# ConvNeXt-V2 block: recomputing three of four row groups in the second stage instead of one of two, with a fixed TensorE order

## The chip, the cores and the metric

The kernel runs on one core of one Trainium2 chip. The metric is the device time of one execution in microseconds (us), as the median of several runs; the profile is one more execution, and its span is a little shorter than the device time. The clock of TensorE is given as the share of its full clock that the profile shows as granted.

## The reference

```python
# x: [1, 512, 512, 96] bf16; dw: [3, 3, 96]; w1: [96, 384]; w2: [384, 96]; all bf16
def reference(x, dw, w1, w2, grn_gamma, grn_beta):
    # 3x3 depthwise convolution over the padded image
    for i in range(K):
        for j in range(K):
            out = out + xp[:, i:i+H, j:j+W, :] * dw[i, j][None, None, None, :]
    h = _layernorm(out, axis=-1)
    h = jnp.einsum('bhwc,ce->bhwe', h, w1)
    h = _gelu(h)
    gx = jnp.sqrt((h * h).sum(axis=(1, 2), keepdims=True) + 1e-6)   # over the whole image
    nx = gx / (gx.mean(axis=-1, keepdims=True) + 1e-6)
    h = grn_gamma * (h * nx) + grn_beta + h
    h = jnp.einsum('bhwe,ec->bhwc', h, w2)
    return x + h
```

The sum over the whole image in `gx` splits the work in two stages. The second matmul needs `gx`, so the hidden tensor (512 x 512 x 384 in bf16, about 201 MB) has to be stored in DRAM and loaded again, or computed twice.

## The kernel before

Stage one goes through the image by rows: convolution on TensorE, layer norm, first matmul, GELU, and the sum of squares on VectorE. Of each block of eight rows it stores the GELU result `g` of the first four to DRAM, and of the other four the smaller normalised input `yn`. Stage two loads `g` for the first four rows, and recomputes matmul and GELU from `yn` for the other four. Then it applies the second matmul with scaled weights `W2s` and adds x. (PE below is TensorE, PEld its weight loads, DVE VectorE, ACT ScalarE and POOL GpSimd. SP only issues DMAs; ACT and POOL issue some beside their own work. `W2s` is w2 scaled by the result of the GRN step, the global response normalisation that needs `gx`.)

```python
GB = 8; GR = 4                       # rows of a block, rows of a group
RECOMP = [(4, 4)]                    # rows 4..7 of each block are recomputed
g_dram  = dram.tile([H // GB, NCH, 128, GB, W], bf16, name="g_dram")    # NCH = 3
yn_dram = dram.tile([H, C, W], bf16, name="yn_dram")
# ... stage one (cut): convolution, layer norm, U = w1.T @ yn, gt = gelu(U), sums of gt*gt ...
            if (r % GB) in recomp_rows:
                nc.sync.dma_start(out=yn_dram[r], in_=yn[:])
# ... in stage_mlp, for each group of four rows and each j of three chunks ...
                    if (rq0 % GB) not in recomp_rows:
                        nc.sync.dma_start(out=g_dram[...], in_=gt[:])       # index cut
# ... GRN step (cut): acc -> ssq -> gx -> tot_ps -> ... -> W2s ...
        gld    = tile_pool(name="gld", bufs=4 * NCH)      # tiles of 8 KB a partition: 96 KB
        ynld   = tile_pool(name="ynld", bufs=3)
        xrpool = tile_pool(name="xr", bufs=6)
        opool  = tile_pool(name="o", bufs=6)
        psO    = tile_pool(name="psO", bufs=4, space=PSUM)
        psU2   = tile_pool(name="psU2", bufs=2, space=PSUM)
        for blk in range(H // GB):
            # load g for rows 0..3 (SP and POOL queues), yn for rows 4..7 (ACT queue)
            for i0 in range(0, n_, 2):               # recompute: 6 times two matmuls, one GELU
                for j in range(NCH):
                    U = psU2.tile([128, ni, W], f32, name="U2")
                    for i in range(ni):
                        nc.tensor.matmul(U[:, i, :], lhsT=w1_sb[...], rhs=ynt[:, i0 + i, :], ...)
                    nc.scalar.activation(out=..., in_=perm_src(U[:]), func=Gelu_apprx_tanh)
            for q in range(GB // GR):
                # xr <- x (POOL queue); xb = xr + bias on VectorE
                for sub in range(NSUB):              # 4 times: 12 matmuls, one VectorE add
                    O = psO.tile([128, GPS, C], f32, name="O")
                    # 4 x 3 matmuls O[:, gl_, :] += g_chunk.T @ W2s[:, j, :]
                    nc.vector.tensor_tensor(out=o_sb[...], in0=O[:], in1=xb[...], op=ALU.add)
                # out <- o_sb (SP and POOL queues by turns)
```

The order of the instructions on each engine is made by a scheduler from this program.

## Time and profile before

| | before |
|---|---|
| device time, median of 4 runs | 2073.48 us |
| span of the profile, mean granted clock of TensorE | 2071.3 us, 0.975 |
| end of the last sum of squares (stage one) | 1467.6 us |
| moved in 1500-2000 us | 392 GB/s |
| ACT busy in 1500-2000 us | 316 of 500 us |

The span in 40 slices (part 2 of the page; busy tenths of ACT and of the DMA engines, and the rate):

```profile
ACT  3788888888888888888888888887476666566565
...
DMA  4644546545446445455445465422799999999996
GB/s 99 161 128 125 153 134 167 150 130 137 141 142 171 139 126 152 127 151 171 129 127 153 128 158 165 126 83 109 245 399 398 395 391 397 389 387 386 386 389 266
```

The last twelve slices are stage two: the rate jumps to some 390 GB/s and stays there, while ACT has a third of its time free. The windows view gives one line for each stretch: its ends, its length, then busy time and count by engine, the granted clock, the DMA share and GB/s.

```profile
core 0: us, PE busy (x) PEld busy (x) DVE busy (x) ACT busy (x) POOL busy (x), PEclk, DMA share, GB/s
600.00:1200.00 600.00, 600.00 (x3699) 338.61 (x3697) 555.36 (x932) 525.00 (x763) 106.76 (x224) 1.00 0.52 144
1500.00:2000.00 500.00, 422.88 (x5979) 314.53 (x5976) 401.73 (x552) 315.83 (x335) 119.00 (x222) 0.97 1.03 392
```

In stage one TensorE has no idle time at clock 1.00. In stage two no compute engine is full. The chain of work that ended last (start us, length us, what) shows what stage two waits for:

```profile
1465.27 2.31 DVE junk L313 x2
...
1842.11 17.89 DMA out_dram<-o_sb
1860.06 19.10 DMA out_dram<-o_sb
1879.25 19.35 DMA out_dram<-o_sb
```

It is the sum of squares on VectorE (junk) to the end of stage one, then one output write of 18-19 us after the other. Longest waits of stage two, 1500-2000 us (in all us, times, longest us):

```profile
...
ACT gl L418 <- PE U L414: 166.3, 73, 6.1
...
DVE o_sb L438 <- DMA out_dram<-o_sb: 58.3, 31, 3.1
...
```

ACT waits for TensorE, and VectorE waits for output writes that free its tiles. The DMA issues (part 6 of the page: count, KB each, median us from issue to landing) show such transfers under load:

```profile
gl<-g_dram SPq DMA_DIRECT2D x128, 512.0 KB, 18.3
...
ynl<-yn_dram ACTq DMA_DIRECT2D x64, 384.0 KB, 14.7
out_dram<-o_sb SPq DMA_DIRECT2D x64, 384.0 KB, 18.4
```

The groups of instructions that cost most in stage two (part 5 of the page: count, busy us and mean ns of one, idle us before them):

```profile
L418 ACT ACTIVATE gl<-U 128x1024 bf16<-128x1024 f32 x384 | 363.9, 1032 | 215.6 <-PE U L414 193.4
...
L438 DVE TENSOR_TENSOR o_sb<-O,xb 128x384 bf16<-128x384 f32 x512 | 257.6, 550 | 119.6 <-DMA out_dram<-o_sb 65.3
...
L414 PE MATMUL U<-ynl,w_sb 96*128 96x512 bf16 x768 | 228.3, 386 | 34.8 <-DMA ynl<-yn_dram 22.0
```

### The profile page before, as it was taken

The numbers are of one execution on the slowest core, as the hardware profiler recorded it, in microseconds if no ns is written. First come the engines' busy times: TensorE is split into PE (matmuls) and PEld (weight loads), VectorE is DVE, ScalarE is ACT, GpSimd is POOL, SyncE is SP. The second block draws the span as 40 slices with busy tenths as digits, with TensorE's granted clock in tenths as the row PEclk, the third lists the DMA queues.
The fourth block names the chain that finished last, engine by engine and source line by source line (L and its number), as shares of the span: only waits on it lengthen the run. The fifth ranks groups of instructions, "written<-read, shape, count | busy, mean of one in ns | idle before, by whom it ended". The sixth has DMA issues, their size and how long they took to land.

```text
span 2071.3 us, 40470 instructions
## 1 busy us (share of the span) xinstructions
PE 1920.5 (93%) x15615; PEld 1162.5 (56%) x15615; DVE 1779.4 (86%) x2849; ACT 1607.4 (78%) x2181; POOL 403.8 (19%) x775
## 2 busy tenths in 40 slices
PE   7999999999999999999999999997498888788887
PEld 4555555555555555555555555552266666566665
DVE  1799999999999999999999999999697878787777
ACT  3788888888888888888888888887476666566565
POOL 0212112112112112111111121124222222222221
PEclk9999999999999999999999999997599999999999
DMA  4644546545446445455445465422799999999996
GB/s 99 161 128 125 153 134 167 150 130 137 141 142 171 139 126 152 127 151 171 129 127 153 128 158 165 126 83 109 245 399 398 395 391 397 389 387 386 386 389 266
DMA packets 432977, 430.35 MB, mean 208 GB/s; under 512 B 313904, under 2 KB 363152, under 8 KB 432784
## 3 DMA queue, kind: packets, MB, share of 16 engines
q1 hardware_dynamic: 382608, 293.53, 46.3%
q0 software_dynamic: 24576, 109.07, 13.5%
q10 hardware_dynamic: 25600, 25.17, 3.7%
q8 instruction: 122, 2.00, 0.4%
q14 instruction: 71, 0.58, 0.1%
HBM read 176.31 MB, written 176.16 MB: 170 GB/s over the span
## 4 chain that ended last, share of the span: by engine, by line
PE 68%; DMA 24%; DVE 3%; issue 3%; ACT 1%; POOL 0%; SPq 0%; POOLq 0%; ACTq 0%; DVEq 0%
PE Y L211 48%; DMA out_dram<-o_sb 21%; PE U L305 15%; PE S L232 2%; DVE junk L313 2%; DMA ynl<-yn_dram 2%; PE T L274 2%; PE O L436 1%; DMA xr<-in_x_dram 1%; DMA xT<-in_x_dram 1%; ACT gl L418 0%; PE U L414 0%; DVE xb L426 0%; DMA gl<-g_dram 0%; DVE o_sb L438 0%
## 5 line engine op out<-in xcount | busy, mean ns | idle before, releaser
L211 PE MATMUL Y<-xT,Dc 96*96 96x511 bf16 (+1 forms) x4602 | 1088.1, 380 | 14.3 <-DMA xT<-in_x_dram 14.3
L313 DVE SCALAR_TENSOR_TENSOR junk<-gt 128x2048 bf16<-128x2048 bf16 x384 | 876.4, 2282 | 78.2 <-ACT gt L310 77.5
L211 PEld LDWEIGHTS <-Dc 96*96 96x96 bf16 x4602 | 563.8, 123 | 443.7 <-DVE Dc L112 10.1
L310 ACT ACTIVATE gt<-U 128x1024 bf16<-128x1024 f32 x768 | 755.2, 1023 | 36.8 <-PE U L305 36.8
L418 ACT ACTIVATE gl<-U 128x1024 bf16<-128x1024 f32 x384 | 363.9, 1032 | 215.6 <-PE U L414 193.4
L281 POOL PARTITION_BROADCAST rbc<-RT x512 | 263.3, 619 | 1173.0 <-DVE ri L246 1060.3
L219 ACT ACTIVATE y_bf<-Y 96x512 bf16<-96x512 f32 x512 | 303.7, 593 | 181.3 <-PE Y L211 181.3
L305 PE MATMUL U<-yn,w_sb 96*128 96x512 bf16 x1536 | 428.0, 387 | 15.1 <-DVE yn L286 8.8
L436 PE MATMUL O<-W2s,gl 128*128 128x96 bf16 x6144 | 348.0, 210 | 76.0 <-DVE o_sb L438 66.1
L436 PEld LDWEIGHTS <-gl 128*128 128x128 bf16 x6144 | 315.5, 100 | 181.1 <-issue 80.7
L438 DVE TENSOR_TENSOR o_sb<-O,xb 128x384 bf16<-128x384 f32 x512 | 257.6, 550 | 119.6 <-DMA out_dram<-o_sb 65.3
L221 ACT ACTIVATE ysq<-Y 96x512 bf16<-96x512 f32 x512 | 298.7, 583 | 0.0
L414 PE MATMUL U<-ynl,w_sb 96*128 96x512 bf16 x768 | 228.3, 386 | 34.8 <-DMA ynl<-yn_dram 22.0
L305 PEld LDWEIGHTS <-w_sb 96*128 96x128 bf16 x1536 | 148.9, 99 | 183.8 <-issue 27.9
L426 DVE TENSOR_TENSOR xb<-xr,B2bc_f 128x1536 f32<-128x1536 bf16 x128 | 224.3, 1753 | 9.7 <-DMA ynl<-yn_dram 7.6
L286 DVE TENSOR_TENSOR yn<-y_bf,rbc 96x512 bf16<-96x512 bf16 x512 | 214.3, 429 | 8.2 <-POOL rbc L281 0.5
L423 POOL DMA_DIRECT2D xr<-in_x_dram x128 | 69.0, 539 | 380.6 <-DVE xb L426 269.5
L414 PEld LDWEIGHTS <-w_sb 96*128 96x128 bf16 x768 | 68.2, 99 | 57.0 <-issue 37.8
L277 DVE CAST RT<-T 128x512 bf16<-128x512 f32 x128 | 86.5, 676 | 0.3 <-PE T L274 0.3
L232 PEld LDWEIGHTS <-ysq 96*128 96x128 bf16 x2048 | 60.7, 96 | 13.5
L232 PE MATMUL S<-ones_c,ysq 96*128 96x1 bf16 x2048 | 60.3, 163 | 0.0
L243 DVE TENSOR_SCALAR var<-S 128x32 f32<-128x32 f32 x64 | 11.6, 181 | 48.8 <-PE S L232 48.8
(51 smaller groups left out, 408.9 us busy)
## 6 DMA issues: line engine op xcount, KB each, us to landing
g_dram<-gt SPq DMA_DIRECT2D x192, 512.0 KB, 3.0
gl<-g_dram SPq DMA_DIRECT2D x128, 512.0 KB, 18.3
xr<-in_x_dram POOLq DMA_DIRECT2D x128, 384.0 KB, 8.3
gl<-g_dram POOLq DMA_DIRECT2D x64, 512.0 KB, 10.1
yn_dram<-yn SPq DMA_DIRECT2D x256, 96.0 KB, 1.7
ynl<-yn_dram ACTq DMA_DIRECT2D x64, 384.0 KB, 14.7
out_dram<-o_sb SPq DMA_DIRECT2D x64, 384.0 KB, 18.4
out_dram<-o_sb POOLq DMA_DIRECT2D x64, 384.0 KB, 10.6
```

The lines of the kernel that those rows point to most:

```text
L211: nc.tensor.matmul(Y[:, oc0:oc1], lhsT=Dc[:, t, :], rhs=xT[0:C, rr + dy, oc0 + dx:oc1 + dx], start=(i == 0), stop=(i == len(taps) - 1),)
L219: nc.scalar.activation(out=y_bf[:], in_=Y[:], func=ACTF.Identity)
L221: nc.scalar.activation(out=ysq[:], in_=Y[:], func=ACTF.Square)
L281: nc.gpsimd.partition_broadcast(rbc[:], RT[32 * i:32 * i + 1, :], channels=128)
L305: nc.tensor.matmul(U[:, kk, :], lhsT=w1_sb[:, j * 128:(j + 1) * 128], rhs=yy[:], start=True, stop=True)
L310: nc.scalar.activation(out=perm_view(gt[:, :], rr0, 2), in_=perm_src(U[:]), func=ACTF.Gelu_apprx_tanh)
L313: nc.vector.scalar_tensor_tensor(out=junk[:], in0=gt[:], scalar=1.0, in1=gt[:], op0=ALU.mult, op1=ALU.mult, accum_out=acc[:, j, quad:quad ...
L414: nc.tensor.matmul(U[:, i, :], lhsT=w1_sb[:, j * 128:(j + 1) * 128], rhs=ynt[:, i0 + i, :], start=True, stop=True)
L418: nc.scalar.activation(out=perm_view(gq, (a_ + i0) % GR, ni), in_=perm_src(U[:]), func=ACTF.Gelu_apprx_tanh)
L426: nc.vector.tensor_tensor(out=xb[:], in0=xr[:], in1=B2bc_f[:, None, :].to_broadcast([128, PXP, C]), op=ALU.add)
L436: nc.tensor.matmul(O[:, gl_, :], lhsT=lhsT, rhs=W2s[:, j, :], start=(j == 0), stop=(j == NCH - 1))
L438: nc.vector.tensor_tensor(out=o_sb[:, sub * GPS:(sub + 1) * GPS, :], in0=O[:], in1=xb[:, sub * GPS:(sub + 1) * GPS, :], op=ALU.add)
```

## The change

The intent is to take bytes off the DMA engines and to give the freed time to TensorE and ACT in a fixed order. Three of four groups are recomputed instead of one of two. TensorE's order in stage two is set by hand: recompute slots (`u_slot`, two matmuls and one GELU) are spread evenly between the `O` matmuls and run 12 slots ahead. The g tiles become smaller: five groups of 3 tiles of 4 KB a partition, 60 KB instead of 96 KB.

```diff
-    RECOMP = [(4, 4)]                                  # cut: block and row bookkeeping
+    RECOMP_PATTERN = [False, True, True, True] if GR == 4 else [False]
-        gld = p2.enter_context(tc.tile_pool(name="gld", bufs=4 * NCH))
-        ynld = p2.enter_context(tc.tile_pool(name="ynld", bufs=3 * max(1, len(RECOMP))))
+        gld = p2.enter_context(tc.tile_pool(name="gld", bufs=5 * NCH))
+        ynld = p2.enter_context(tc.tile_pool(name="ynld", bufs=4))
+        LEAD = 12
+        AHEAD = 5 - 1
+        def u_slot(q, i0, j):
+            alloc_upto(q)
+            if q not in ynt_of:
+                ynt_of[q] = ynld.tile([C, GR, W], bf16, name="ynl")
+                nc.scalar.dma_start(out=ynt_of[q][:], in_=yn_dram[q * GR:q * GR + GR].rearrange("r c w -> c r w"))
+            ...                                        # two matmuls, one GELU
+        def pump(b):
+            target = min(n_u, b * n_u // n_b + LEAD)
+            while u_done[0] < target:
+                u_slot(*u_slots[u_done[0]])
+                u_done[0] += 1
+        with tc.manual_schedule(engines={mybir.EngineType.PE}):
+            for q in range(NGRP):
+                alloc_upto(q + AHEAD)                  # g loads four groups ahead
+                ...
                 for sub in range(NSUB):
+                    pump(q * NSUB + sub)
                     ...                                # 12 O matmuls, one VectorE add
```

Of stage one only the stores are changed: in the two traces the order of the compute instructions is the same on every engine up to 1405 us.

## The prediction

> **What bounds the kernel now.** Two stages, read from the windows view. Up to about 1410 us TensorE is busy without a break (600.00 of 600 us in 600-1200) at granted clock 1.00. Until 1467 us VectorE works off its sum-of-squares backlog (the chain shows junk steps of 2.3 us each). The second stage runs to 2071 us; from 1500 to 2000 us DMA bounds it: every slice at 9, 195.8 MB moved, mean 392 GB/s, and the chain is a row of 17-20 us output writes. The Trainium skill, "DMA: Bandwidth & Descriptors", Specifications, puts the fabric ceiling at 435 GB/s; this trace tops out near 400. The stage moves (page part 6) 192x512 KB of g, 64x384 KB of yn, 128x384 KB each of x and output: about 226 MB, 578 us at 392 GB/s. ACT has slack: it waits 166 us on U2 matmuls in 1500-2000.
>
> **What the change does.** Three of four row groups are recomputed instead of one of two. In stage two g loads fall from 192 to 96 (-50 MB), yn loads rise from 64 to 96 (+12.6 MB): 189 MB, 481 us at 392 GB/s. GELUs rise from 384 to 576 and U2 matmuls from 768 to 1152. PE order is fixed by hand: two U2 matmuls between each twelve O matmuls, four every eighth time, twelve U slots ahead. In stage one g writes halve and yn writes grow by half; the order of PE, ACT and DVE instructions there is unchanged and PE bounds it: no gain.
>
> **Costs in stage two after (estimates from this trace).**
> - ACT: uninterrupted GELUs pitch 0.91-0.94 us (9 in 8.35 us). 576 x 0.93 = 536 us.
> - PE: 0.216 us per U2 matmul (the Trainium skill, "TensorE: Matmul & The Clock Gate", Back-to-back issue gap, gives N/2.4 + 2.5 ns = 216 ns; 4 in 1.03 us here agrees) and 0.043 us per O matmul (44 issued in 1.88 us): 1152 x 0.216 + 6144 x 0.043 = 513 us.
> - VectorE unchanged: 257.6 + 224.3 = 482 us. DMA 481 us.
>
> So the bound moves from DMA (578) to ACT (536), PE close behind. ACT waits for PE, PE for ACT's two U2 buffers and VectorE's four O buffers, in a fixed order: I add 2-4% (8-20 us). The first O cannot start before about 1490 us (W2s, first g loads), as now. 1490 + 530 + coupling 8-20 + drain 10-12 gives about 2040 us.
>
> **Prediction.** 2040 us, 8 in 10 between 2022 and 2062. Chances: faster by over 2% (below 2032) 0.30; within 2% 0.68; slower 0.02. The gain, 33 us, is a third of the 97 us of DMA time removed; the rest is hidden by the new ACT/PE bound.
>
> **What would show each step.**
> - Windows: stage one ends at 1465-1470 us, PE fully busy at clock 1.00.
> - In 1500-2000 DMA falls to 340-360 GB/s; g loads land in under 18 us; the chain holds PE and ACT, not output writes.
> - ACT busy there rises from 64% to about 95%, PE to 90% or more; GELU mean still 1.03 us.
> - A group of four rows takes 4.2-4.35 us (now about 4.5).
>
> **What would make it wrong.**
> - Slower: the fixed PE order stalls on late g or yn data[...].
> - Slower: output writes and g loads, in order on SP, run late though the DMA engines are free.
> - Faster: ACT pitch 0.91, U slots starting 10 us before W2s is ready, almost no coupling: about 2020.
> - Stage one could gain a little from halved g writes, if DMA matters there.

## More of the kernel before

Last, the start of stage two in the timeline (start us, length us, in brackets the idle time before it and what ended it). Only the loads of x, the scaled weights and the first GELU are shown:

```profile
1467.89 3.54 POOL L423 DMA_DIRECT2D xr<-in_x_dram  x6 [9.69 <-DVE junk L313]
...
1481.72 0.56 DVE L370 TENSOR_SCALAR W2s<-w_sb,sc 128x96 bf16<-128x96 bf16 x3
...
1483.67 1.94 ACT L418 ACTIVATE gl<-U 128x1024 bf16<-128x1024 f32 x2
```

The loads of x waited for the last sum of squares (junk), whose memory their tiles reuse by the order of the pools, and `W2s` came 14 us after the end of stage one.

## The result

The changed kernel takes 2024.38 us (median of 8 runs, 2022.93 to 2026.23); the kernel before takes 2072.91 us (median of 13). The ratio is 0.9766, 95% interval 0.9756 to 0.9775. (A ratio here is the mean time of one kernel's runs over that of the other's of the same rounds, so not quite the ratio of the quoted medians.) It is 2.3% faster, 48.5 us by the medians. The profiled execution: span 2024.4 us, clock 0.983.

The slices of the kernel after, same rows as before:

```profile
ACT  3788888888888888888888888888589999999998
...
DMA  4644444554444454444345444441389999999996
GB/s 97 146 106 106 122 121 112 131 118 106 106 129 117 115 131 111 108 106 137 108 123 131 102 108 108 136 105 57 100 279 358 359 350 357 348 352 356 357 347 245
```

ACT is now full in stage two. The DMA row still shows 9 almost everywhere, at some 40 GB/s less: the busy share alone doesn't tell which of the two kernels is bound by DMA. The windows of the kernel after (columns as before):

```profile
600.00:1200.00 600.00, 600.00 (x3699) 338.58 (x3697) 555.58 (x932) 524.98 (x763) 106.81 (x224) 1.00 0.46 119
1500.00:2000.00 500.00, 487.64 (x6813) 348.33 (x6810) 449.43 (x598) 498.27 (x538) 119.12 (x222) 1.00 1.03 354
```

Stage one is as it was. In 1500-2000 us ACT is busy 498.27 of 500 us with 538 GELUs, so one takes 0.926 us. The chain after:

```profile
1465.35 2.31 DVE junk L299 x2
...
1514.65 2.85 ACT gl L409 x3
1547.99 2.85 ACT gl L409 x3
...
1707.26 16.37 DMA ynl<-yn_dram
...
2008.38 7.67 issue
```

Stage one ends at the same time. The row of output writes is gone; stage two repeats itself exactly, every 33.34 us for eight groups (1514.65 to 1547.99), or 4.17 us a group. A few waits for yn loads remain. Waits in 1500-2000 us:

```profile
...
PE U L407 <- ACT gl L409: 10.9, 60, 0.2
...
ACT gl L409 <- PE U L407: 1.6, 2, 1.2
...
```

TensorE waits 10.9 us for ACT to free a U2 tile, and ACT waits 1.6 us for TensorE. This is the picture of an ACT-bound stage in which nobody else is late. DMA issues:

```profile
ynl<-yn_dram ACTq DMA_DIRECT2D x96, 384.0 KB, 9.2
gl<-g_dram SPq DMA_DIRECT2D x48, 512.0 KB, 8.3
...
out_dram<-o_sb SPq DMA_DIRECT2D x64, 384.0 KB, 6.5
```

The g loads on SP land in 8.3 instead of 18.3 us, the writes on SP in 6.5 instead of 18.4. The groups on ACT and TensorE:

```profile
L409 ACT ACTIVATE gl<-U 128x1024 bf16<-128x1024 f32 x576 | 534.4, 1027 | 4.2 <-PE U L407 4.1
...
L407 PE MATMUL U<-ynl,w_sb 96*128 96x512 bf16 x1152 | 348.7, 384 | 22.8 <-ACT gl L409 17.0
```

The 192 added GELUs cost their full time: ACT's busy time in this group went from 363.9 to 534.4 us, and its idle time before them from 215.6 to 4.2 us. The start of stage two after:

```profile
1459.20 3.54 POOL L432 DMA_DIRECT2D xr<-in_x_dram  x6 [0.92 <-PE U L291]
...
1474.30 0.56 DVE L353 TENSOR_SCALAR W2s<-w_sb,sc 128x96 bf16<-128x96 bf16 x3
...
1476.25 1.94 ACT L409 ACTIVATE gl<-U 128x1024 bf16<-128x1024 f32 x2
```

The loads of x start 8.7 us earlier and no longer after a junk step; `W2s` is ready and the first GELU starts 7.4 us earlier. This was not foreseen.

### The profile page after: what moved, and what is told of

It reads as the page before. It is cut to its first block, busy times and chain, and to the rows that moved or that the text cites. A ratio compares the mean times of both kernels' runs of the same rounds, so it can differ in the third digit from the quotient of the medians.

```text
span 2024.4 us, 41508 instructions
## 1 busy us (share of the span) xinstructions
PE 1959.3 (97%) x15999; PEld 1173.9 (58%) x15999; DVE 1794.2 (89%) x2849; ACT 1778.0 (88%) x2373; POOL 395.5 (20%) x759
## 4 chain that ended last, share of the span: by engine, by line
PE 80%; ACT 8%; issue 5%; DVE 3%; DMA 3%; POOL 1%; SPq 0%; ACTq 0%; POOLq 0%; DVEq 0%
PE Y L197 48%; PE U L291 15%; ACT gl L409 8%; PE U L407 6%; PE O L445 6%; DVE junk L299 2%; PE S L218 2%; DMA ynl<-yn_dram 2%; PE T L260 2%; DMA xT<-in_x_dram 1%; DMA gl<-g_dram 0%; POOL xr L432 0%; ACT gt L296 0%; POOL out_dram L450 0%; DVE xb L435 0%
## 5 line engine op out<-in xcount | busy, mean ns | idle before, releaser
L409 ACT ACTIVATE gl<-U 128x1024 bf16<-128x1024 f32 x576 | 534.4, 1027 | 4.2 <-PE U L407 4.1
L407 PE MATMUL U<-ynl,w_sb 96*128 96x512 bf16 x1152 | 348.7, 384 | 22.8 <-ACT gl L409 17.0
L447 DVE TENSOR_TENSOR o_sb<-O,xb 128x384 bf16<-128x384 f32 x512 | 266.5, 552 | 64.3 <-PE O L445 62.3
L291 PEld LDWEIGHTS <-w_sb 96*128 96x128 bf16 x1536 | 148.9, 99 | 183.9 <-issue 27.9
L407 PEld LDWEIGHTS <-w_sb 96*128 96x128 bf16 x1152 | 86.2, 99 | 55.9 <-issue 46.5
```

The lines of the kernel that those rows point to most:

```text
L291: nc.tensor.matmul(U[:, kk, :], lhsT=w1_sb[:, j * 128:(j + 1) * 128], rhs=yy[:], start=True, stop=True)
L407: nc.tensor.matmul(U[:, i, :], lhsT=w1_sb[:, j * 128:(j + 1) * 128], rhs=ynt[:, i0 + i, :], start=True, stop=True)
L409: nc.scalar.activation(out=perm_view(gts_of[q][j][:, :], i0, 2), in_=perm_src(U[:]), func=ACTF.Gelu_apprx_tanh)
L447: nc.vector.tensor_tensor(out=o_sb[:, sub * GPS:(sub + 1) * GPS, :], in0=O[:], in1=xb[:, sub * GPS:(sub + 1) * GPS, :], op=ALU.add)
```

## The experiments

All runs were correct. Each was timed against the kernel before on the same chip; that kernel's median lay between 2071.94 and 2073.77 us. All outputs are right. The changed kernel was not run again, so a distance from its 2024.38 us under about 2 us is not read as an effect. The first theory (A) is that bytes bound stage two before, and that cutting them is the gain. Its first rival (B) is that the hand-made order is the gain.

### The fixed order with half of the groups recomputed

```diff
-    RECOMP_PATTERN = [False, True, True, True] if GR == 4 else [False]
+    RECOMP_PATTERN = [False, True]
-        LEAD = 12
+        LEAD = 8
```

> The changed kernel, but one of two row groups recomputed as before (226 MB in stage two again); PE order by hand kept, lead cut from 12 to 8 U slots so that the five gl buffers suffice. Theory A (the bytes: stage two of before was DMA-bound, the cut in bytes is the gain): DMA bound again near 392 GB/s in 1500-2000, output writes in the chain, total 2055 to 2070 us, 0.2 to 0.8% faster than before (the earlier start of some 7 us stays). Theory B (the hand-made order and deeper leads removed waits, bytes hardly matter): with only 384 GELUs ACT needs 356 us, VectorE 482 us, so total 2000 us or less.

Measured: 2059.19 us, ratio 0.9941 (0.9924 to 0.9957). Its windows line for 1500-2000 us (columns as before):

```profile
1500.00:2000.00 500.00, 420.22 (x5976) 318.81 (x5972) 409.80 (x556) 326.35 (x333) 134.86 (x251) 0.90 1.03 395
```

DMA moves 395 GB/s, as with the scheduler's order, and ACT has 174 us free. Two quite different orders with the same bytes run at the same rate, so B fails: the order alone is worth little while the bytes stay. Of the 12.75 us that this run gains, up to 8.3 are not the order's: the first GELU of stage two starts at 1475.38 instead of 1483.67 us in its trace, as in the changed kernel. Theory A holds for the kernel before.

### Three of four groups recomputed, scheduler's order

```diff
-        with tc.manual_schedule(engines={mybir.EngineType.PE}):
+        if True:
```

> The changed kernel without the hand-made PE order: the scheduler orders TensorE as in before; three of four groups recomputed. Theory A (bytes): DMA no longer binds, ACT does; 2024 to 2040 us, most of the gain stays. Theory B (order): PE stalls return, ACT busy in 1500-2000 falls from 498 of 500 us to under 450, total 2060 us or more.

Measured: 2149.54 us, ratio 1.0372 (1.0356 to 1.0387), slower than the kernel before. So A alone fails too: with the order left to the scheduler the higher share of recomputation gains nothing and costs 77 us. In 1500-2000 us ACT was busy 405 us and DMA moved 287 GB/s, so neither was full. The windows line, and one gap in the timeline:

```profile
1500.00:2000.00 500.00, 445.78 (x5593) 303.53 (x5590) 368.41 (x489) 405.45 (x440) 97.83 (x182) 1.00 0.84 287
...
1710.24 2.93 PE L445 MATMUL O<-W2s,gl 128*128 128x96 bf16 x65
...
1710.44 2.22 ACTq L403 DMA_DIRECT2D ynl<-yn_dram  x3
...
1715.19 1.02 PE L407 MATMUL U<-ynl,w_sb 96*128 96x512 bf16 x4 [0.49 <-DMA ynl<-yn_dram]
...
1715.88 2.85 ACT L409 ACTIVATE gl<-U 128x1024 bf16<-128x1024 f32 x3 [4.29 <-PE U L407]
```

The scheduler put three yn loads together in ACT's queue, directly before the GELUs that need them. Meanwhile TensorE ran 65 and then 15 O matmuls in one go. When the first U2 matmul could start, ACT had been idle for 4.29 us. Of ACT's idle time in 1500-2000 us the trace puts 56.7 us down to yn loads and 35.2 us to U2 matmuls. Which of the two did the harm, the late loads or the bunched matmuls, this run doesn't tell; a later one goes part of the way.

### Two of three groups recomputed

```diff
-    RECOMP_PATTERN = [False, True, True, True] if GR == 4 else [False]
+    RECOMP_PATTERN = [False, True, True]
```

> The changed kernel with two of three groups recomputed (510 GELUs instead of 576; about 202 MB in stage two instead of 189). If the changed kernel is bound by ACT at 0.926 us per GELU and DMA can still move 392 GB/s, stage two is bound by DMA at about 515 us against ACT's 472: 2002 to 2012 us, faster than the changed kernel. If the changed kernel is already at the limit of the DMA engines (its page shows 9 in every DMA slice at 354 GB/s), 2030 to 2055 us.

Measured: 2034.44 us, ratio 0.9810 (0.9793 to 0.9827), 10 us slower than the changed kernel and inside the rival's range. The DMA engines moved 371 GB/s in 1500-2000 us and the yn loads took 18.5 us to land. Waits there:

```profile
...
ACT gl L409 <- PE U L407: 54.7, 46, 4.0
...
PE U L407 <- DMA ynl<-yn_dram: 36.7, 24, 3.5
...
```

Stage two waits for loads again, at a lower mean rate than the 392-395 GB/s of the kernels that recompute half. In 40 slices of these 500 us the rate swings between 265 and 401 GB/s (371 to 406 in the kernel before), so the lower mean may come from gaps in what is asked for and not from slower transfers; deeper pools for two thirds were not tried. With these pools the ratio of three in four is not far on the ACT side of the balance, as the estimate had it, but near it.

### The g pool as large as before

```diff
-        gld = p2.enter_context(tc.tile_pool(name="gld", bufs=5 * NCH))
+        gld = p2.enter_context(tc.tile_pool(name="gld", bufs=8 * NCH))
```

> The changed kernel with 24 instead of 20 gl buffers of 4 KB a partition, so that the tiles behind them (ynl, xr) lie where they lay in before, on memory that the last sum-of-squares tiles (gt, junk) use; the program loads g no further ahead. Theory C (layout: the first x and yn loads started 8 us earlier in the changed kernel only because the smaller gl pool moved their tiles onto memory that comes free earlier): first yn load at about 1467 instead of 1459.6 us, W2s ready at 1479 to 1483 instead of 1475 us, total 2028 to 2033 us. Rival: the start is set by something else; 2023 to 2026 us.

(The expectation miscounts: NCH is 3, so these are 24 tiles instead of 15. And the yn loads of the changed kernel start at 1458.6 us, not 1459.6.) Measured: 2033.39 us, ratio 0.9810 (0.9796 to 0.9825), 9.0 us slower than the changed kernel. The start of its stage two in the timeline:

```profile
1467.61 3.54 POOL L432 DMA_DIRECT2D xr<-in_x_dram  x6 [9.69 <-DVE junk L299]
...
1480.74 0.55 DVE L353 TENSOR_SCALAR W2s<-w_sb,sc 128x96 bf16<-128x96 bf16 x3
...
1482.69 1.94 ACT L409 ACTIVATE gl<-U 128x1024 bf16<-128x1024 f32 x2
```

The loads of x wait for junk again, and W2s and the first GELU are back within 1 us of where they were before. The later GELU explains 6.4 of the 9.0 us; its stage is also slower by 0.12 us per eight groups (33.45 us), which makes 1.9 us over the 16 of them. The total lies 0.4 us above the range of theory C, far outside the rival's. So about 9 us of the result come with the smaller pool, a side effect of where tiles lie, at least for the 6.4 us of the start. Without them the ratio is 0.981, and the gain is no longer clearly above 2%.

### The changed kernel with longer runs in the yn loads

```diff
-    yn_dram = dram.tile([H, C, W], bf16, name="yn_dram")
+    yn_dram = dram.tile([H // GR, C, GR, W], bf16, name="yn_dram")
-                nc.sync.dma_start(out=yn_dram[r], in_=yn[:])
+                nc.sync.dma_start(out=yn_dram[r // GR, :, r % GR, :], in_=yn[:])
-                nc.scalar.dma_start(out=ynt_of[q][:], in_=yn_dram[q * GR:q * GR + GR].rearrange("r c w -> c r w"))
+                nc.scalar.dma_start(out=ynt_of[q][:], in_=yn_dram[q])
```

> The changed kernel with yn kept in DRAM group by group, so that a yn load reads 4 KB runs instead of 1 KB runs; nothing else. Theory A1 (the changed kernel is bound by ACT in stage two, the DMA engines only look full): total unchanged, 2020 to 2026 us, ACT still 498 of 500 us in 1500-2000; DMA share there falls below 1.00 and yn loads land faster than 9.2 us. Theory A2 (it sits on the DMA limit as well): 5 us faster or more.

Measured: 2024.05 us, ratio 0.9758 (0.9733 to 0.9783); the changed kernel has 0.9766. Windows line for 1500-2000 us:

```profile
1500.00:2000.00 500.00, 489.11 (x6841) 349.60 (x6839) 450.77 (x601) 499.87 (x541) 119.22 (x223) 1.00 1.01 354
```

The yn loads land in 7.0 instead of 9.4 us in this stretch, and the total doesn't move: ACT is busy 499.87 of 500 us. A1 holds. Only the DMA share stayed at 1.01 where less than 1.00 was expected; that row does not measure what is left.

### Two of three groups with longer runs

The diffs of the two-thirds kernel and of the one before, together.

> Two of three groups recomputed, with 4 KB runs in the yn loads. Theory D (the 1 KB runs of the yn loads cost DMA time out of proportion: while DMA is full the rate falls from 395 GB/s at 11% yn bytes to 371 at 17% and 354 at 20%): the DMA bound of the two-thirds kernel is lifted, 395 GB/s or more, limits ACT 472, VectorE 482, DMA about 500 us: 1985 to 2010 us. Rival (the length of runs does not matter, the two-thirds kernel is simply at the limit of bytes): 2028 to 2036 us as without it.

Measured: 2032.58 us, ratio 0.9791 (0.9753 to 0.9829), as without the longer runs (2034.44 us). The rate stayed at 369 GB/s. The waits moved from yn loads (8.3 us to landing now) to g loads (39.7 us of TensorE's waits). Theory D, that short runs lower the rate, fails.

### The kernel before with longer runs

The same change of `yn_dram` in the kernel before.

> The kernel before with 4 KB runs in the yn loads; nothing else. Theory A (stage two of before bound by DMA) with theory D (1 KB runs expensive): 10 to 40 us faster, 2035 to 2062 us, at 400 GB/s or more. Without D: 2068 to 2076 us. If stage two of before were bound by its instruction order and not by DMA: no change either, but DMA share below 1.00.

Measured: 2067.19 us, ratio 0.9967 (0.9934 to 1.0000), at 394 GB/s. This is neither the gain of theory D nor quite no change; D fails here as well.

### Scheduler's order, yn loads asked for early and on SP

```diff
-        with tc.manual_schedule(engines={mybir.EngineType.PE}):
+        if True:
-        ynld = p2.enter_context(tc.tile_pool(name="ynld", bufs=4))
+        ynld = p2.enter_context(tc.tile_pool(name="ynld", bufs=6))
         def alloc_upto(qmax):
             ...
+                else:
+                    ynt_of[q] = ynld.tile([C, GR, W], bf16, name="ynl")
+                    nc.sync.dma_start(out=ynt_of[q][:], in_=yn_dram[q * GR:q * GR + GR].rearrange("r c w -> c r w"))
```

> Three of four groups recomputed, the scheduler's order on TensorE (as in the run without the hand-made order, 2149 us), but the yn loads are asked for four groups ahead and issued from SP, so that ACT's queue holds no loads. Theory E1 (the scheduler's version lost its time because yn loads stood last in ACT's own queue, directly before their use): ACT idle in 1500-2000 falls from 95 us to under 30 us and the total to 2025 to 2060 us. Theory E2 (the bunching of U2 and O matmuls on TensorE lost it): 2100 us or more, with ACT waiting for PE.

Measured: 2040.44 us, ratio 0.9834 (0.9802 to 0.9867). The windows line for 1500-2000 us:

```profile
1500.00:2000.00 500.00, 486.85 (x6670) 349.26 (x6669) 439.65 (x583) 491.50 (x533) 116.35 (x217) 0.99 1.02 345
```

ACT was busy 491.5 of 500 us, as E1 expected. So of the 125 us (2149.54 - 2024.38) that the scheduler's order cost, 109 us come back when only the yn loads are changed. E2 is not excluded as the way in which they were lost: in this trace TensorE's order is regular as well. In 1500-2000 us no run of O matmuls is longer than 12, where the scheduler's first version has runs of up to 80, with 42% of its O matmuls in runs of 30 or more. Whether the late loads held ACT up directly, or through the order that the scheduler made around them, stays open. Asking for them earlier, keeping six tiles and moving them to SP were done together; which of these was needed is open too. The other 16 us are not the hand-made order alone, since here the yn loads share SP's queue, where the g loads now land in 15.1 instead of 8.3 us. The traces show one merit of the hand-made order beside its regularity: most loads of the changed kernel stand 17 to 19 GELUs ahead of their use in ACT's queue. In the kernel before it was 12 or 13, in the scheduler's version of three in four 0, 6 or 12.

### The pools of stage two in another order

```diff
-        gld, ynld, xrpool, opool = ...     # opened in this order (shortened here)
+        opool, ynld, xrpool, gld = ...
```

> The changed kernel with the pools of stage two opened in another order (output tiles first, then yn, x, and the gl tiles last), so that neither the yn, x nor gl tiles lie on the small tiles of the GRN step; nothing else. Theory C (start set by where tiles lie): the first GELU of stage two no longer waits for W2s (1476.25 us) but only for the square root of the GRN step (about 1469 us), and since ACT binds stage two the total falls by 4 to 7 us: 2017 to 2021 us. Rival (the start of ACT is not what the end follows, TensorE or DMA is): 2023 to 2026 us.

Measured: 2019.33 us, ratio 0.9736 (0.9722 to 0.9751), 5.1 us faster than the changed kernel and the fastest of all. The first GELU of stage two in its timeline, and W2s after it:

```profile
1469.48 1.94 ACT L409 ACTIVATE gl<-U 128x1024 bf16<-128x1024 f32 x2
...
1473.80 0.56 DVE L353 TENSOR_SCALAR W2s<-w_sb,sc 128x96 bf16<-128x96 bf16 x3
```

The first GELU no longer waits for W2s and starts at 1469.48 instead of 1476.25 us. Most of these 6.8 us arrive in the total, as they should where ACT is what the end follows.

### Two of three groups, yn loads by turns in two ranges of partitions

```diff
+        # two padded copies of w1 (rows 0-95 or 32-127), four cleared yn tiles of 128 partitions
+                v = b_ % 2
+                nc.scalar.dma_start(out=ynt_of[q][32 * v:32 * v + C, :, :], in_=...)
-            nc.tensor.matmul(U[:, i, :], lhsT=w1_sb[:, j * 128:(j + 1) * 128], ...)
+            nc.tensor.matmul(U[:, i, :], lhsT=w1z[ynv_of[q]][:, j * 128:(j + 1) * 128], ...)
```

> Two of three groups recomputed; yn loads land by turns in partitions 0-95 and 32-127, with zero-padded weights and a contraction over all 128 partitions. Theory P (the rate falls with the share of yn bytes because their 96 partitions use the SBUF ports unevenly; the Trainium skill, SBUF page, gives the odd ports only partitions 64-127): the uneven load is gone, 385 GB/s or more in 1500-2000 and 10 us or more faster than the control of the same call. Without P: equal to the control within 4 us, at about 370 GB/s.

Measured: 2029.03 us, ratio 0.9785 (0.9770 to 0.9800). The control has `v = 0` throughout:

> The control of the run before it: the same padded weights and the same cleared tiles, but all yn loads in partitions 0-95. Expected 2032 to 2042 us (the two-thirds kernel, 2034 us, and up to 5 us for clearing the tiles), at about 370 GB/s. Theory P says nothing more about it; a value below 2025 us would mean that the padding itself changes something.

Measured: 2032.21 us, ratio 0.9799 (0.9782 to 0.9815). Both moved 375 GB/s. The difference of 3.2 us is within the 4 us that were named as no effect, and the intervals overlap. Theory P, in the size expected, fails; each single load still lay in 96 partitions, so only the sum over loads was made even. Why the rate is lower when more of the bytes are yn stays open.

### A lead of six slots

```diff
-        LEAD = 12
+        LEAD = 6
```

> The changed kernel with a lead of 6 U slots instead of 12; nothing else. Theory F (TensorE and ACT did not hold each other up because the long lead has every GELU ready before its O matmuls; the order alone would not do): O matmuls now wait for GELUs, ACT loses about 0.3 us or more per four groups, less 2.8 us for a shorter tail: 2027 to 2040 us, ACT busy in 1500-2000 below 494 us. Rival (the two U2 buffers and the regular order suffice, the lead only lengthens the tail): 2020 to 2023 us, ACT still 498 us.

Measured: 2035.77 us, ratio 0.9821 (0.9807 to 0.9834), 11.4 us slower than the changed kernel. ACT was busy 493.99 of 500 us. At one place in four groups this is seen in its timeline:

```profile
1702.82 0.60 PE L445 MATMUL O<-W2s,gl 128*128 128x96 bf16 x10 [0.15 <-ACT gl L409]
...
1703.89 1.02 ACT L409 ACTIVATE gl<-U 128x1024 bf16<-128x1024 f32 x1 [0.21 <-PE U L407]
```

The O matmuls wait 0.15 us for a GELU, the next U2 pair comes after them, and ACT then idles 0.21 us for it. F holds: the long lead is what keeps the two engines from waiting for each other. Not all of the 11.4 us is such waiting in the steady run. In the traces the 21st GELU is already 2.5 us later than in the changed kernel, the last one 11.3 us: with six slots in front, the first O matmul comes at 1481.19 us, and TensorE then waits 2.6 us for g loads, with ACT behind it.

## Why the prediction was right, and where it was off

- **Stage two of before was bound by DMA.** Right. Two orders with the same bytes ran at 392 and 395 GB/s, with ACT free for 174-184 of 500 us.
- **Stage one gains nothing.** Right: the last junk step starts at 1465.27 before and at 1465.35 us after.
- **The bound moves to ACT.** Right. ACT is busy 498.27 of 500 us, relief for DMA changed nothing (2024.05 us), and an earlier or later first GELU moves the total (2019.33, 2033.39 us). The estimate of 0.93 us for a GELU met 0.926 us.
- **The sum was too large by three terms.** The prediction counted 1490 for the first O matmul, 530 for the O matmuls, 8-20 for coupling and 10-12 for the drain. With midpoints that is 2045 us, so 2040 already lay low in its own sum. In the trace the first full run of O matmuls starts at 1487.54, the last ends at 2018.94 and the span ends at 2024.4 us: 1487.5 + 531.4 + 5.5.
  - The **coupling** term ("I add 2-4% (8-20 us)") is the step that failed most: 531.4 us were measured for 530 plus coupling, so 1.4 us. By part 5 of the page, ACT was idle for only 4.2 us in all before its 576 GELUs. The run with half the lead shows what holds it down: there the total rises by 11.4 us. The prediction saw that U slots run twelve ahead, but used it only in its list of what would make it wrong. Of the three things named there for "about 2020", "almost no coupling" is the one that happened.
  - The **drain** was 5.5 instead of 10-12 us.
  - The **start** ("about 1490 us, as now") came 2.5 us earlier, and its reason was wrong, so that the number was near is luck. The prediction let the first O matmul wait for W2s and g loads. In the trace with a lead of six the first g loads are in by 1484.08 us, and W2s starts at 1474.30 us in the changed kernel; what comes last before its first O is the twelve U slots. With the pools in another order W2s starts only 0.50 us earlier (1473.80), but the first GELU 6.8 us and the first O 5.65 us (1481.89). Behind this lies a term that the prediction missed: the first GELU came 7.4 us earlier because the smaller g pool moved other tiles to memory that is free sooner. Put back, it costs 9.0 us.
- **The gain of 33 us was 48.5 us.** The chance given to more than 2% was 0.30, to within 2% 0.68; the result is just beyond that line, and the time lies inside the range. It crosses the line with the side effect of the pool, which nobody planned: without its 9.0 us the gain would be 39.5 us.
- **The order was held to be a risk, not a need.** "The fixed PE order stalls on late g or yn data" was the fear. The opposite was measured: with the scheduler's order the same bytes take 2149.54 us, and 2040.44 us once the yn loads are asked for early and on SP.
- **Signs named in advance.** DMA at 340-360 GB/s (354), g loads under 18 us (8.3), chain of PE and ACT, PE over 90% (487.64 of 500 us), GELU mean 1.03 us (1027 ns): as said. ACT at "about 95%" was 99.7%. A group at 4.2-4.35 us was 4.17.

Not explained is why the mean rate drops from 392-395 GB/s with half of the groups recomputed to 369-375 with two thirds. Neither the length of the runs nor the range of partitions, as they were varied here, accounts for it; gaps in the requests were not tested.

## What to carry to other kernels

Fewer bytes pay only if the freed time can be used: here the change of ratio needed loads that stand far ahead of their use, and without them it lost 77 us against the kernel before. When two engines hand tiles to each other in a fixed order, look at the lead before adding a charge for mutual waiting: 12 slots made it nearly zero, 6 cost 11 us, some 2.5 of them at the start. And a changed pool size moves its neighbours: ask at every stage border which earlier tile's memory the first loads reuse.

## What the Trainium skill lacked or had wrong

- "DMA: Bandwidth & Descriptors", Specifications, gives a fabric ceiling of 435 GB/s. Stage two ran at 392-395 GB/s where DMA bound it with half of the groups recomputed, and at 369-375 with two thirds. No page read here says what lowers it; that it is the mix of transfers is not shown.
- "SBUF — State Buffer", the section on the DMA port swizzle, lets one expect that loads into partitions 0-95 load the ports unevenly. Spreading them over 0-95 and 32-127 by turns changed 375 GB/s to 375 GB/s and the total by 3.2 us, with overlapping intervals. Each single load stayed uneven, so this tests only the sum over loads.
- "TensorE: Matmul & The Clock Gate", Back-to-back issue gap, gives about 131 ns for N=512 in a real stream of weight load and matmul, and 216 ns for the isolated gap. The streams here follow the second: four U2 matmuls take 1.03 us with the last one's 0.38 us in it, so (1.03 - 0.38) / 3 = 0.217 us each.
- No page read here names the danger of loads in a compute engine's own queue: with three yn loads placed directly before the GELUs that use them, ACT was idle 95 of 500 us, of which the trace puts 56.7 us down to these loads.
